# ScalarE's Sign for the weights of the first product, and one low part of three moved to VectorE

## The chip, the core and the metric

The kernel runs on one core of one Trainium2 chip (trn2). The metric is the device time of one execution in microseconds: 970.57 us, the median of 3 runs (970.44 to 973.05), before the change.

## What is computed

A gated linear attention over 4 batches, 8 heads, 768 positions and heads of 48, then two products of a multilayer kind. The weights reach the kernel as 64-bit floats.

```python
state = alpha[:, :, t, :, None] * state + einsum('bhd,bhe->bhde', k[:, :, t], v[:, :, t])
y[:, :, t] = einsum('bhd,bhde->bhe', q[:, :, t], state)      # 768 steps; x = y as 3072 x 384
x = ((x @ w_a) * (x @ w_b)) @ w_out                          # 384 -> 1536 -> 384, "the first product"
h = x @ w_in
out = (h * cos(h)) @ w_out2                                  # 384 -> 2048 -> 384
```

## The kernel before

**Tiles and stages.** The 3072 tokens are worked in six groups of 512. Attention goes in 24 chunks of 128 positions; the four chunks of the first group are worked before anything else, and each later group's chunks are worked between the matmuls of the group ahead of it. The first product takes 12 blocks f of its hidden 1536 (128 columns each). A step (g, f) issues `s1`: two products `pa` and `pb` (w_a and w_b of block f, 9 matmuls each of 128x512), and, two steps later (`LAG`), `s2`: the block's share of the output `po` (w_out, 9 matmuls). Nine and not three, because every operand is split into a high part that TensorE's fp32r form holds and a low part: `mm3` (L196 to L199) does low times high, high times low, high times high. After the six groups the second pair of products follows in the same manner (`s3`, `s4`).

**Weights.** Each 128x384 block of weights is loaded as 32-bit pairs (`raw_w`, L100): word 0 holds the low 32 bits of each float, word 1 the high 32. They are decoded on the chip, once, during the first group; afterwards they stay in SBUF. Blocks under `W2` = 36 belong to the first product (w_a and w_b of a block f, and w_out of block f - 2, come together as three); the 32 blocks from `W2` on belong to the second. The stages of the decoding, each named by a letter in the order string of a step, are

- r: ScalarE scales the low word to a small integer (`rest`, L106),
- s: VectorE takes the top two bits of the high word and ors them with it (`sign`, L111). For 17 of the 36 blocks (`banked`) ScalarE writes the small integer to a PSUM bank instead (L168), and VectorE reads it there (L169),
- n: VectorE shifts the high word left by 3 and clears its top two bits (`shift`, L126),
- a: GpSimd adds the two words as integers (`rounded`, L132): the result is the fp32 value,
- h: ScalarE casts it to the high part (`dec_h`, L190),
- l: GpSimd subtracts the high part from the value (`dec_l`, L194): the low part. The first two blocks alone have it on VectorE (letter d).

Per step three blocks of later steps go through these stages, and

```python
ORDER1 = 'sbpcrnadhlmw'
```

is the order in which a step of the first product writes its work out: s, then the scans of the next attention chunk (p, `att_pre`: L242, L250 and two products L246, L252 on VectorE), the eviction of `pa` on ScalarE (c, `s1_mid`, L437), r, n, a, d, h, l, the product of `pa` and `pb` on VectorE and its cast on ScalarE (m, `s1_mul`, L442 and L444), the low part of the step before (w, `s1_low`, L449). Behind these come the attention parts of the step: at steps 2, 4, 6, 8 (`POS0`) the scores of a chunk (`att_a`, its mask L287, and a copy L279), at steps 3, 5, 7, 9 its output (`att_b`: on ScalarE L308 and the splits L393, on VectorE L339 and L394) and one or two range checks of alpha on ScalarE (`att_chk`, L265). Engines work their own list strictly in this order (`tc.manual_schedule`). For the steps before the first `s1` the order is the string `START`, where s3, r4 and so on are the same letters with a negative step.

**Buffers.** PSUM tiles of the pool `ps` (pa, pb, the attention's tiles, and the `low` tiles of `banked` blocks) share five banks. With two steps' pa and pb among them, `pb` of a step takes the bank of `pb` of the step before, which is free when that step's L442 has read it.

**Constants.** `check1` compares the smallest absolute high word of the first product's weights with `TINY`; if any check failed, a general path (`general`) would be run behind everything else. `s1_mid` copies pa to SBUF; `s2_out` copies the result of the first product (L467).

Of the kernel before, what the change touches and what calls it, by code (L numbers as in the profile page):

```python
# [6 lines left out]
F32 = mybir.dt.float32  # L7
BF16 = mybir.dt.bfloat16
F32R = mybir.dt.float32r
I32 = mybir.dt.int32  # L10
U32 = mybir.dt.uint32
AF = mybir.ActivationFunctionType
ALU = mybir.AluOpType
# [4 lines left out]
P = 128  # L18
# [7 lines left out]
DM = H * D  # L26
FF1 = 1536
FF2 = 2048
NF1 = FF1 // P
# [6 lines left out]
ORDER1 = 'sbpcrnadhlmw'  # L36
ORDER2 = "scywrbnamdp"
POS0 = (2, 4, 6, 8)
LOV = 3
ND = 2  # L40
START = 'A0 P1 M0 w5 D0 A1 P2 Y0 M1 X0 D1 r4 x0 w6 A2 P3 M2 Y1 X1 s3 b3 r3 D2 n3 s2 a2 A3 M3 Y2 b2 n2 h2 d2 Y3 X2 r2 x1 X3 s1 b1 a1 n1 h1 L0 l1 r1 D3'
SPARE = 5
# [5 lines left out]
F_LOW = 1e-14  # L48
F_MIN = 1e-25
TINY = 2.0 ** -15  # L50


@with_exitstack
def tile_kernel(ctx, tc, al, qk, vt, vz, wts, mask, qr, vr, out):
# [48 lines left out]
    def rest(raw):  # L103
        if wide:
            lo32 = raw[:, :, 0]
            nc.scalar.activation(lo32.bitcast(I32), lo32, AF.Copy, scale=2.0 ** -29)  # L106

    def sign(raw):
        if wide:
            lo32, hi32 = raw[:, :, 0], raw[:, :, 1]  # L110
            nc.vector.scalar_tensor_tensor(out=lo32, in0=hi32, scalar=0xC0000000, in1=lo32, op0=ALU.bitwise_and, op1=ALU.bitwise_or)  # L111
# [39 lines left out]
        raws[i] = raw_w(i, wpool, "w")  # L151


    banked = set()

    def dec_r(*blocks):
        for i in blocks:
            if i not in banked:
                rest(raws[i])

    def dec_s(*blocks):
        for i in blocks:
            if i not in banked:
                sign(raws[i])
                continue
            t = ps.tile([P, DM], I32, name=f"low{i}", tag="ps")
            lo32, hi32 = raws[i][:, :, 0], raws[i][:, :, 1]
            nc.scalar.activation(t, lo32, AF.Copy, scale=2.0 ** -29)  # L168
            nc.vector.scalar_tensor_tensor(out=lo32, in0=hi32, scalar=0xC0000000, in1=t.bitcast(U32), op0=ALU.bitwise_and, op1=ALU.bitwise_or)  # L169

    def dec_b(*blocks):
        for i in blocks:
# [3 lines left out]
    def dec_n(*blocks):  # L176
        for i in blocks:
            if i >= W2:
                least(raws[i])
        for i in blocks:  # L180
            shift(raws[i])

    def dec_a(*blocks):
        for i in blocks:
# [249 lines left out]
    def s1_mid(g, f, T):  # L434
        pab = abt[g, f]
        a_sb = work.tile([P, 512], F32, name=f"asb{g}_{f}", tag="asb", bufs=2)
        nc.scalar.copy(a_sb[:, :T], pab[0][:, :T])  # L437
        abt[g, f] = (pab, a_sb)

    def s1_mul(g, f, T):  # L440
# [23 lines left out]
    def s2_out(g, t0, T):  # L464
        for o in range(KT):
            xo = att.tile([P, 512], F32, name=f"xo{g}_{o}", tag="a", bufs=3)
            nc.scalar.copy(xo[:, :T], po1[o][:, :T])  # L467
            nc.sync.dma_start(out=x2d[:, o, t0:t0 + T], in_=xo[:, :T])


# [92 lines left out]
    def check1():  # L563
        nc.vector.tensor_reduce(out=okc[:, 0:1], in_=stats[:, 0:1], axis=AX.XY, op=ALU.add)
        nc.vector.tensor_reduce(out=okc[:, 1:2], in_=stats[:, 1:4], axis=AX.XY, op=ALU.add)
        nc.vector.scalar_tensor_tensor(out=okc[:, 0:1], in0=okc[:, 1:2], scalar=0.0, in1=okc[:, 0:1], op0=ALU.mult, op1=ALU.add)
        nc.vector.tensor_scalar(out=okc[:, 1:2], in0=okc[:, 0:1], scalar1=0.0, scalar2=None, op0=ALU.is_equal)
        if wide:
            nc.vector.tensor_reduce(out=okc[:, 2:3], in_=wmin, axis=AX.X, op=ALU.min)
            nc.vector.tensor_scalar(out=okc[:, 2:3], in0=okc[:, 2:3], scalar1=TINY, scalar2=None, op0=ALU.is_ge)  # L570
            nc.vector.tensor_tensor(out=okc[:, 1:2], in0=okc[:, 1:2], in1=okc[:, 2:3], op=ALU.mult)

    def check2():
# [119 lines left out]
    for m, bl in seq:  # L693
# [5 lines left out]
            at(ld_at, m, load_raw, order[nl])  # L699
            nl += 1  # L700
        d = 1 if m < NF1 else 0
        if wide and 1 <= m < NF1 and m - 1 not in POS0:
            banked.update(bl)
        at(r_at, m - 1 - d, dec_r, *bl)
        at(s_at, m - d, dec_s, *bl)
        at(b_at, m - d, dec_b, *bl)
# [178 lines left out]
```

## Time and profile before

| what | value |
| --- | --- |
| median of 3 runs | 970.57 us |
| the profiled execution, first to last instruction (span) | 967.5 us |
| around it (970.57 - 967.5) | 3.1 us |
| TensorE busy in the span | 941.5 us, 97% |
| VectorE, ScalarE, GpSimd busy | 627.7, 491.0, 194.3 us |
| mean granted TensorE clock | 0.994 |

The span is that of one profiled execution; no device time of that execution alone is given beside it, so the 3.1 us are the difference to the median of the runs. Busy times are sums over the span: a TensorE that is 97% busy over the whole can still stand idle in one stretch, and the stretch is where the reading has to start.

### The profile page before, as it was taken

Reading aid. Unit: us, or ns where it says so; the run is one execution under the profiler, and the core shown is the slowest. Engines: PE = TensorE matmul, PEld = TensorE weight load, DVE = VectorE, ACT = ScalarE, POOL = GpSimd, SP = SyncE. Lnnn points to the kernel's source line nnn. Section 1 sums busy time; section 2 is a strip of 40 time slices with the busy share of each in tenths; the row PEclk is TensorE's granted clock in tenths of the full one; section 3 lists DMA queues with packets and bytes.
Section 4 is the critical chain, followed back from the end, with each engine's and each line's share of the span. In section 5 each row is a group of like instructions: output and inputs, shape, how many; then the busy total and the mean of one; then the engine's idle time right before and its main releaser. Section 6 shows DMA issues by size and latency. Waiting matters only on the chain.

```text
span 967.5 us, 14093 instructions
## 1 busy us (share of the span) xinstructions
PE 941.5 (97%) x5215; PEld 765.8 (79%) x5215; DVE 627.7 (65%) x1000; ACT 491.0 (51%) x1039; POOL 194.3 (20%) x184
## 2 busy tenths in 40 slices
PE   7879999999999999999999999999999999999996
PEld 5757788888888888888888878788888888888885
DVE  7999955454553556444259998766666666666664
ACT  2656633323332324233256777666566666665653
POOL 5788820000000000000037764201001000010000
PEclk9999999999999999999999999999999999999999
DMA  9765214341433333030145530010010100200001
GB/s 281 240 222 178 74 40 142 102 142 46 149 109 100 115 126 98 23 103 14 59 144 154 174 131 1 1 65 1 1 66 1 66 1 0 66 1 1 34 0 37
DMA packets 41982, 79.98 MB, mean 83 GB/s; under 512 B 6192, under 2 KB 13360, under 8 KB 41904
## 3 DMA queue, kind: packets, MB, share of 16 engines
q1 hardware_dynamic: 41760, 78.72, 25.7%
q8 instruction: 43, 0.70, 0.3%
q14 instruction: 35, 0.29, 0.1%
q10 hardware_dynamic: 144, 0.26, 0.1%
HBM read 67.36 MB, written 9.44 MB: 79 GB/s over the span
## 4 chain that ended last, share of the span: by engine, by line
PE 83%; DMA 5%; DVE 5%; ACT 3%; issue 1%; POOL 1%; SPq 1%; DVEq 0%; ACTq 0%; POOLq 0%
PE pq L198 6%; PE pq L199 6%; PE ph L199 6%; PE ph L197 6%; PE ph L198 6%; PE pq L197 6%; PE po L197 5%; PE po L198 5%; PE po L199 5%; PE pb L197 5%; PE pb L198 5%; PE pa L198 5%; PE pa L197 4%; PE pa L199 4%; PE pb L199 4%; DMA w<-wts 3%
## 5 line engine op out<-in xcount | busy, mean ns | idle before, releaser
L442 DVE TENSOR_TENSOR asb<-pb,asb 128x512 f32<-128x512 f32 x72 | 49.7, 690 | 161.1 <-PE pb L199 118.2
L132 POOL TENSOR_TENSOR w<-w 128x384 int32<-128x384 int32 x68 | 65.6, 986 | 400.4 <-DVE w L126 395.9
L198 PE MATMUL pq<-g,w 128*128 128x512 f32 x288 | 112.8, 392 | 2.2 <-DVE g L524 2.2
L444 ACT CAST ab<-asb 128x512 fp32r<-128x512 f32 x72 | 44.8, 622 | 133.4 <-DVE asb L442 133.4
L197 PE MATMUL pq<-g,w 128*128 128x512 f32 x288 | 112.3, 390 | 0.0
L199 PE MATMUL pq<-g,w 128*128 128x512 f32 x288 | 112.2, 390 | 0.0
L197 PE MATMUL ph<-x,w 128*128 128x512 f32 x288 | 112.2, 389 | 0.0
L199 PE MATMUL ph<-x,w 128*128 128x512 f32 x288 | 112.1, 389 | 0.0
L198 PE MATMUL ph<-x,w 128*128 128x512 f32 x288 | 112.0, 389 | 0.0
L499 DVE SCALAR_TENSOR_TENSOR r<-r,ph 128x512 f32<-128x512 f32 x96 | 66.1, 688 | 66.2 <-ACT r L498 65.7
L437 ACT COPY asb<-pa 128x512 f32<-128x512 f32 x72 | 42.1, 585 | 126.9 <-PE pa L199 126.8
L497 ACT ACTIVATE r<-r 128x512 f32<-128x512 f32 x96 | 60.8, 633 | 83.9 <-DVE r L493 83.9
L492 DVE SCALAR_TENSOR_TENSOR r<-n,ph 128x512 f32<-128x512 int32 x96 | 65.9, 687 | 47.6 <-ACT n L490 47.6
L194 POOL TENSOR_TENSOR w<-w,w 128x384 fp32r<-128x384 f32 x66 | 89.8, 1382 | 27.0 <-ACT w L190 23.9
L197 PE MATMUL pb<-xg,w 128*128 128x512 f32 x216 | 84.4, 391 | 6.0 <-DVE asb L442 4.6
L197 PE MATMUL po<-ab,w 128*128 128x512 f32 x216 | 88.8, 411 | 0.0
L197 PE MATMUL pa<-xg,w 128*128 128x512 f32 x216 | 84.2, 390 | 2.0 <-DVE w L169 1.1
L198 PE MATMUL po<-ab,w 128*128 128x512 f32 x216 | 84.7, 392 | 0.0
L199 PE MATMUL po<-ab,w 128*128 128x512 f32 x216 | 84.7, 392 | 0.0
L198 PE MATMUL pa<-xg,w 128*128 128x512 f32 x216 | 84.2, 390 | 0.1
L198 PE MATMUL pb<-xg,w 128*128 128x512 f32 x216 | 84.1, 389 | 0.0
L199 PE MATMUL pa<-xg,w 128*128 128x512 f32 x216 | 84.1, 389 | 0.0
(110 smaller groups left out, 1867.0 us busy)
## 6 DMA issues: line engine op xcount, KB each, us to landing
w<-wts SPq DMA_DIRECT2D x104, 384.0 KB, 4.0
al<-al SPq DMA_DIRECT2D x24, 226.2 KB, 4.4
k<-qk SPq DMA_DIRECT2D x24, 224.0 KB, 3.8
q<-qk SPq DMA_DIRECT2D x24, 224.0 KB, 3.6
x2d<-xo SPq DMA_DIRECT2D x18, 256.0 KB, 2.2
x2f<-x2d SPq DMA_DIRECT2D x18, 256.0 KB, 3.6
out_t<-yo SPq DMA_DIRECT2D x17, 256.0 KB, 2.1
v<-vt SPq DMA_DIRECT2D x22, 192.0 KB, 2.8
```

The costliest lines, as they stand in the source:

```text
L132: nc.gpsimd.tensor_tensor(out=hi32, in0=hi32, in1=lo32, op=ALU.add)
L194: e.tensor_tensor(out=wt[i][:, 1, :], in0=raws.pop(i), in1=wt[i][:, 0, :].bitcast(F32), op=ALU.subtract)
L197: nc.tensor.matmul(o, wlo, xhi, start=start, stop=False)
L198: nc.tensor.matmul(o, whi, xlo, start=False, stop=False)
L199: nc.tensor.matmul(o, whi, xhi, start=False, stop=stop)
L437: nc.scalar.copy(a_sb[:, :T], pab[0][:, :T])
L442: nc.vector.tensor_tensor(out=a_sb[:, :T], in0=pab[1][:, :T], in1=a_sb[:, :T], op=ALU.mult)
L444: nc.scalar.copy(ab[:, 0, :T], a_sb[:, :T])
L492: nc.vector.scalar_tensor_tensor(out=r, in0=n, scalar=-C1, in1=p, op0=ALU.mult, op1=ALU.add)
L497: nc.scalar.activation(r, r, AF.Sin, scale=0.5)
L499: nc.vector.scalar_tensor_tensor(out=r, in0=r, scalar=1.0, in1=p, op0=ALU.subtract, op1=ALU.mult, reverse0=True)
```

## The change

For the 36 blocks of the first product:

- ScalarE writes the small integer of the low word as 16 bits into the lower half of word 0 (`low`), in place; no block goes through PSUM any more (`banked` is gone).
- ScalarE's Sign of the high word, as bf16, goes into the upper half of word 0 (`sgn`), at the letter s. Its 1.0 or -1.0 has the bits of an fp32 number's sign and exponent; VectorE's `sign` (L111, L169) is gone for these blocks.
- VectorE's shift (`up`) is one operation, without the mask of the top bits. With the integer sum of both words the value comes out as half of the weight. So `s1_mid` and `s2_out` scale by 4 and by 2 with the copy that they make anyway, and the bound in `check1` is `SMALL`, twice `TINY`.
- `LOV` is 2: of three low parts GpSimd makes two; the third (w_out's) goes to VectorE, one step later, at the letter d. That moves 10 subtractions.

The second product's blocks (from `W2`) are decoded as before.

```diff
--- before.py
+++ after.py
@@ -8,6 +8,7 @@
 BF16 = mybir.dt.bfloat16
 F32R = mybir.dt.float32r
 I32 = mybir.dt.int32
+I16 = mybir.dt.int16
 U32 = mybir.dt.uint32
 AF = mybir.ActivationFunctionType
 ALU = mybir.AluOpType
@@ -36,7 +37,7 @@
 ORDER1 = 'sbpcrnadhlmw'
 ORDER2 = "scywrbnamdp"
 POS0 = (2, 4, 6, 8)
-LOV = 3
+LOV = 2
 ND = 2
 START = 'A0 P1 M0 w5 D0 A1 P2 Y0 M1 X0 D1 r4 x0 w6 A2 P3 M2 Y1 X1 s3 b3 r3 D2 n3 s2 a2 A3 M3 Y2 b2 n2 h2 d2 Y3 X2 r2 x1 X3 s1 b1 a1 n1 h1 L0 l1 r1 D3'
 SPARE = 5
@@ -48,6 +49,7 @@
 F_LOW = 1e-14
 F_MIN = 1e-25
 TINY = 2.0 ** -15
+SMALL = 2.0 ** -14
 
 
 @with_exitstack
@@ -151,22 +153,26 @@
         raws[i] = raw_w(i, wpool, "w")
 
 
-    banked = set()
+    def low(raw):
+        if wide:
+            nc.scalar.activation(raw.bitcast(I16)[:, :, 0], raw[:, :, 0], AF.Copy, scale=2.0 ** -29)
+
+    def sgn(raw):
+        if wide:
+            nc.scalar.activation(raw.bitcast(BF16)[:, :, 1], raw[:, :, 1].bitcast(F32), AF.Sign)
+
+    def up(raw):
+        if wide:
+            x = raw[:, :, 1]
+            nc.vector.tensor_scalar(out=x, in0=x, scalar1=3, scalar2=None, op0=ALU.logical_shift_left)
 
     def dec_r(*blocks):
         for i in blocks:
-            if i not in banked:
-                rest(raws[i])
+            (rest if i >= W2 else low)(raws[i])
 
     def dec_s(*blocks):
         for i in blocks:
-            if i not in banked:
-                sign(raws[i])
-                continue
-            t = ps.tile([P, DM], I32, name=f"low{i}", tag="ps")
-            lo32, hi32 = raws[i][:, :, 0], raws[i][:, :, 1]
-            nc.scalar.activation(t, lo32, AF.Copy, scale=2.0 ** -29)
-            nc.vector.scalar_tensor_tensor(out=lo32, in0=hi32, scalar=0xC0000000, in1=t.bitcast(U32), op0=ALU.bitwise_and, op1=ALU.bitwise_or)
+            (sign if i >= W2 else sgn)(raws[i])
 
     def dec_b(*blocks):
         for i in blocks:
@@ -178,7 +184,7 @@
             if i >= W2:
                 least(raws[i])
         for i in blocks:
-            shift(raws[i])
+            (shift if i >= W2 else up)(raws[i])
 
     def dec_a(*blocks):
         for i in blocks:
@@ -434,7 +440,7 @@
     def s1_mid(g, f, T):
         pab = abt[g, f]
         a_sb = work.tile([P, 512], F32, name=f"asb{g}_{f}", tag="asb", bufs=2)
-        nc.scalar.copy(a_sb[:, :T], pab[0][:, :T])
+        nc.scalar.activation(a_sb[:, :T], pab[0][:, :T], AF.Copy, scale=4.0 if wide else 1.0)
         abt[g, f] = (pab, a_sb)
 
     def s1_mul(g, f, T):
@@ -464,7 +470,7 @@
     def s2_out(g, t0, T):
         for o in range(KT):
             xo = att.tile([P, 512], F32, name=f"xo{g}_{o}", tag="a", bufs=3)
-            nc.scalar.copy(xo[:, :T], po1[o][:, :T])
+            nc.scalar.activation(xo[:, :T], po1[o][:, :T], AF.Copy, scale=2.0 if wide else 1.0)
             nc.sync.dma_start(out=x2d[:, o, t0:t0 + T], in_=xo[:, :T])
 
 
@@ -567,7 +573,7 @@
         nc.vector.tensor_scalar(out=okc[:, 1:2], in0=okc[:, 0:1], scalar1=0.0, scalar2=None, op0=ALU.is_equal)
         if wide:
             nc.vector.tensor_reduce(out=okc[:, 2:3], in_=wmin, axis=AX.X, op=ALU.min)
-            nc.vector.tensor_scalar(out=okc[:, 2:3], in0=okc[:, 2:3], scalar1=TINY, scalar2=None, op0=ALU.is_ge)
+            nc.vector.tensor_scalar(out=okc[:, 2:3], in0=okc[:, 2:3], scalar1=SMALL, scalar2=None, op0=ALU.is_ge)
             nc.vector.tensor_tensor(out=okc[:, 1:2], in0=okc[:, 1:2], in1=okc[:, 2:3], op=ALU.mult)
 
     def check2():
@@ -699,8 +705,6 @@
             at(ld_at, m, load_raw, order[nl])
             nl += 1
         d = 1 if m < NF1 else 0
-        if wide and 1 <= m < NF1 and m - 1 not in POS0:
-            banked.update(bl)
         at(r_at, m - 1 - d, dec_r, *bl)
         at(s_at, m - d, dec_s, *bl)
         at(b_at, m - d, dec_b, *bl)
```

Three places show how the instructions move. In the names, w is a block's raw words or its split parts, low a PSUM tile, asb and ab the product of pa and pb.

VectorE between steps 3 and 4, before (L394 the splits of chunk 4, L111 letter s, L126 letter n, L442 letter m):

```order
L394 TENSOR_TENSOR xg_853<-py_1_821,xg_853 112x128
L111 SCALAR_TENSOR_TENSOR w_690<-w_690 128x384
L111 SCALAR_TENSOR_TENSOR w_692<-w_692 128x384
L111 SCALAR_TENSOR_TENSOR w_694<-w_694 128x384
L126 TENSOR_SCALAR w_690<-w_690 128x384
L126 TENSOR_SCALAR w_692<-w_692 128x384
L126 TENSOR_SCALAR w_694<-w_694 128x384
L442 TENSOR_TENSOR asb_4_915<-pb_4_890,asb_4_915 128x512
```

and in the changed kernel (L400 the splits, L167 the shift, L200 a low part, L448 the product):

```order
L400 TENSOR_TENSOR xg_843<-py_1_811,xg_843 112x128
L167 TENSOR_SCALAR w_683<-w_683 128x384
L167 TENSOR_SCALAR w_685<-w_685 128x384
L167 TENSOR_SCALAR w_687<-w_687 128x384
L200 TENSOR_TENSOR w_802<-w_571,w_802 128x384
L448 TENSOR_TENSOR asb_4_905<-pb_4_880,asb_4_905 128x512
```

Three instructions are gone ahead of the product, and one has come: the low part of a block whose value and high part were made a step earlier.

ScalarE at the same place, before (L393 the splits, L265 the range checks, L437 the eviction of pa, L190 letter h):

```order
L393 ACTIVATE xg_853,stats<-py_1_821 112x128
L265 ACTIVATE junk,stats<-g_789,lim 112x516
L265 ACTIVATE junk,stats<-g_634,lim 112x516
L437 COPY asb_4_915<-pa_4_880 128x512
L190 CAST w_923<-w_619 128x384
```

and in the changed kernel (L162 is the Sign, L158 the 16-bit low word, L443 the eviction):

```order
L399 ACTIVATE xg_843,stats<-py_1_811 112x128
L271 ACTIVATE junk,stats<-g_779,lim 112x516
L271 ACTIVATE junk,stats<-g_627,lim 112x516
L162 ACTIVATE w_683<-w_683 128x384
L162 ACTIVATE w_685<-w_685 128x384
L162 ACTIVATE w_687<-w_687 128x384
L443 ACTIVATE asb_4_905<-pa_4_870 128x512
L158 ACTIVATE w_770<-w_770 128x384
```

Three Signs now stand between the range checks and the eviction; the low words of three blocks, which before went to PSUM in the step after, are made here, in place.

GpSimd, two rounds of the letters a and l before (L132 the sum, L194 the low part):

```order
L132 TENSOR_TENSOR w_568<-w_568 128x384
L194 TENSOR_TENSOR w_807<-w_564,w_807 128x384
L194 TENSOR_TENSOR w_809<-w_566,w_809 128x384
L194 TENSOR_TENSOR w_811<-w_568,w_811 128x384
L132 TENSOR_TENSOR w_619<-w_619 128x384
```

and in the changed kernel (L134 the sum, L200 the low part):

```order
L134 TENSOR_TENSOR w_571<-w_571 128x384
L200 TENSOR_TENSOR w_798<-w_567,w_798 128x384
L200 TENSOR_TENSOR w_800<-w_569,w_800 128x384
L134 TENSOR_TENSOR w_618<-w_618 128x384
```

The third subtraction has left GpSimd's list; the sums follow one instruction sooner.

## Rows read from the trace of the kernel before

**Rows 1.** The page: TensorE's busy tenths in 40 slices, about 24 us each.

```profile
PE   7879999999999999999999999999999999999996
```

**Rows 2.** Windows: stretch, length, busy us (count) by engine, granted clock, DMA.

```profile
34.40:112.00 77.60, 67.39 (x410) 52.05 (x411) 72.87 (x115) 47.82 (x122) 65.53 (x54) 0.98 0.59 188
112.00:475.00 363.00, 363.00 (x2375) 295.66 (x2374) 185.93 (x317) 119.23 (x324) 16.11 (x13) 1.00 0.29 90
52.30:55.20 2.90, 2.90 (x10) 2.32 (x9) 2.90 (x4) 1.20 (x4) 2.90 (x3) 0.51 1.03 402
```

**Rows 3.** Timeline, TensorE, 34 to 112 us: start, length, instruction, [idle before, releaser].

```profile
34.40 0.47 PE L197 MATMUL pa<-xg,w 128*128 128x512 f32 x1 [0.90 <-ACT xg L393]
...
40.22 0.47 PE L197 MATMUL pa<-xg,w 128*128 128x512 f32 x1 [1.10 <-DVE w L169]
...
50.30 1.16 PE L272 MATMUL pa<-q,k 48*128 48x128 f32 x16 [1.64 <-DVE q L252]
...
70.53 0.47 PE L197 MATMUL pb<-xg,w 128*128 128x512 f32 x1 [1.14 <-DVE asb L442]
...
106.40 0.47 PE L197 MATMUL pb<-xg,w 128*128 128x512 f32 x1 [1.64 <-DVE asb L442]
```

**Rows 4.** Timeline, VectorE: the products L442 of steps 1 to 7.

```profile
50.97 0.69 DVE L442 TENSOR_TENSOR asb<-pb,asb 128x512 f32<-128x512 f32 x1
...
58.99 0.68 DVE L442 TENSOR_TENSOR asb<-pb,asb 128x512 f32<-128x512 f32 x1
...
69.71 0.68 DVE L442 TENSOR_TENSOR asb<-pb,asb 128x512 f32<-128x512 f32 x1
...
75.96 0.68 DVE L442 TENSOR_TENSOR asb<-pb,asb 128x512 f32<-128x512 f32 x1
...
86.47 0.68 DVE L442 TENSOR_TENSOR asb<-pb,asb 128x512 f32<-128x512 f32 x1
...
95.50 0.68 DVE L442 TENSOR_TENSOR asb<-pb,asb 128x512 f32<-128x512 f32 x1
...
105.58 0.68 DVE L442 TENSOR_TENSOR asb<-pb,asb 128x512 f32<-128x512 f32 x1
```

**Rows 5.** Timeline, VectorE, from the first product's start to the step 1 product.

```profile
34.85 3.06 DVE L111 SCALAR_TENSOR_TENSOR w<-w 128x384 uint32<-128x384 uint32 x3
...
39.54 1.47 DVE L169 SCALAR_TENSOR_TENSOR w<-w,low 128x384 uint32<-128x384 uint32 x3
...
43.52 1.49 DVE L169 SCALAR_TENSOR_TENSOR w<-w,low 128x384 uint32<-128x384 uint32 x3 [1.10 <-ACT low L168]
44.92 1.66 DVE L242 TENSOR_TENSOR_SCAN g<-al,one_end 112x516 f32<-112x516 f32 x1
...
50.16 0.90 DVE L126 TENSOR_SCALAR w<-w 128x384 uint32<-128x384 uint32 x3
```

**Rows 6.** Timeline, VectorE: three shifts with GpSimd at work, beside those at 50.16.

```profile
92.19 3.38 DVE L126 TENSOR_SCALAR w<-w 128x384 uint32<-128x384 uint32 x3
```

**Rows 7.** Timeline, ScalarE: two waits, the check ahead of step 4's eviction, three low words.

```profile
28.43 0.83 ACT L314 COPY sbd<-ts 48x96 f32<-48x96 f32 x3 [1.08 <-DVE ts L305]
...
39.70 0.53 ACT L168 ACTIVATE low<-w 128x384 int32<-128x384 uint32 x1 [3.80 <-issue]
...
74.24 0.73 ACT L265 ACTIVATE junk<-g,lim 112x516 uint8<-112x516 f32 x1
...
79.83 1.44 ACT L106 ACTIVATE w<-w 128x384 int32<-128x384 uint32 x3
```

**Rows 8.** Groups by line and shape: busy us, mean ns of one | idle before.

```profile
L116 ACT ACTIVATE w<-w 128x384 f32<-128x384 f32 x32 | 17.5, 559 | 16.9 <-DVE w L111 16.8
...
L265 ACT ACTIVATE junk<-g,lim 112x516 uint8<-112x516 f32 x24 | 17.4, 725 | 0.1
```

**Rows 9.** The same view, VectorE.

```profile
L194 DVE TENSOR_TENSOR w<-w,w 128x384 fp32r<-128x384 f32 x2 | 2.3, 1184 | 0.0
...
L394 DVE TENSOR_TENSOR xg<-py,xg 128x384 fp32r<-128x384 f32 x2 | 1.0, 543 | 0.0
```

## The prediction

> **What bounds the kernel now.** I read the slices of the page first: TensorE shows a 9 in every slice from the fifth to the last but one, and 7, 8, 7 or 8 only in the first ones [rows 1]. The windows say the same in microseconds: from 112 to 475 us TensorE is busy for all of 363.00 us, from 34.40 to 112.00 us for 67.39 of 77.60 [rows 2]. So what ScalarE, VectorE and GpSimd do matters only in the first group of 512 tokens, while the weights are decoded, and the most that can be had there is 77.60 - 67.39 = 10.2 us of waits, and what a low clock costs. The third window gives that: between 52.30 and 55.20 us the granted clock is 0.51, the lower of TensorE's two levels (1.2 against 2.4 GHz), right behind the wait of 1.64 us at 50.30 [rows 2, 3]. Half of those 2.9 us, about 1.4 us, would not be needed at the upper level. The weights of the second product are decoded around 500 to 600 us as before and drop out of the reckoning.
>
> Next the timeline of TensorE for who ends its waits. At 40.22 us it is VectorE's L169, that is, a PSUM bank that holds a low word; at 50.30 us the scaled q of chunk 4; at 70.53 and 106.40 us, and at two more places (steps 3 and 7), it is the product L442 of the step before, which gives back the bank of pb [rows 3]. In all four, pb starts 0.14 us behind L442's end: 69.71 + 0.68 = 70.39, and 70.53; 105.58 + 0.68 = 106.26, and 106.40 [rows 3, 4]. The wait at 106.40 is the last one of any size. **So the end moves by as much as the L442 of step 7, at 105.58, moves**, as long as TensorE's own work does not become later than it. That row is what I follow, from L442 to L442 [rows 4]: the distances are 8.02, 10.72, 6.25, 10.51, 9.03 and 10.08 us for steps 1 to 7. The long ones (even to odd steps) hold the scans of a chunk on VectorE, the short ones its splits.
>
> **Part 1: up to the L442 of step 1.** VectorE loses L111 at 34.85, L169 at 39.54 and L169 at 43.52 with its wait of 1.10 [rows 5]: 3.0 + 1.4 + 2.5 = 6.9 us on a VectorE that is otherwise nearly without gaps there. The Signs go to ScalarE. For a Sign I take 0.47 us: three of L106 take 1.44 [rows 7], and Abs on the same shape has 559 ns for one against an overlap of about 0.1 [rows 8]. No row shows a 16-bit result at every eighth byte; the nearest below is that 0.47, the nearest above the range check with its 8-bit result, 725 ns on 516 columns [rows 8]. Beside that price: the Trainium skill (ScalarE: Activation LUTs, section on what ACT_TABLE_LOAD costs) gives 280 ns + 0.833 ns per element for an ACTIVATE whose bias is a pointer, overlapping the next by about 93 ns. By that page a Sign would be 0.60 us long and 0.51 apart, an estimate; the sum would lose 0.7 us by it.
>
> Ahead of the first product ScalarE gets four Signs, 1.9 us. It waits 1.08 us there for VectorE at 28.43 [rows 7], and VectorE comes sooner by two L111; I take +0.4 us for the first matmul (bounds 0 and 1.9): 34.8. Behind it ScalarE has three Signs, two casts, three low words and three Signs, 11 times 0.47 = 5.2 us, until 40.0. Before, it stood 3.80 us idle for a PSUM bank in this stretch [rows 7], and that idle time pays for the Signs. So the L442 of step 0 starts near 40.7, the scans at 41.3; from the scan at 44.92 to the shifts at 50.16 is 5.24 us [rows 5], so they end at 46.5; three shifts (0.8) and the new low part follow. Its price lies between 0.54 us (L394, one operand in PSUM) and 1.18 us (the same subtraction on VectorE with GpSimd at work) [rows 9]; I take the middle, 0.85, because GpSimd works in part of the stretch. L442 of step 1: 48.2 against 50.97, **-2.8 us**. The waits at 40.22 and 50.30 and the low clock go with it, which is why TensorE can follow.
>
> **Part 2: the loops.** Even to odd (three of them): three L169 go (1.40 from start to the next start, 43.52 to 44.92 [rows 5]), a low part comes: -1.40 + 0.85 = -0.55 each, **-1.65**. The Signs lie under the scans there. Odd to even: here the Signs are a new wait, since the shift overwrites the word that Sign reads, and ScalarE comes to them only behind the splits and the range checks. In step 3 to 4 the second check starts at 74.24 and ends near 74.97 [rows 7], 5.26 us after the L442 at 69.71; three Signs to 6.67, the last shift to 7.0, the low part to 7.8. That is +1.55 against 6.25; the same 7.8 in step 5 to 6, also with two checks, is -1.2 against 9.03. From step 1 to 2 there are no splits: about 2.15 us to the end of one check, 1.4 for the Signs, 0.3 and 0.85: 4.7, **-3.3** against 8.02. Together -1.65 + 1.55 - 1.2 - 3.3 = **-4.6**. The 9.03 is long because its three shifts took 3.38 us beside GpSimd [rows 6] where those at 50.16 took 0.90 [rows 5]; such a round took place in two of seven steps. GpSimd has 10 of 34 subtractions fewer here, but will still meet shifts: I leave half a round, **+1.2**.
>
> **What costs nothing.** The scale in the copies of pa and of the result replaces a copy by one with a factor, covered by a full TensorE after 112 us [rows 2]; the 17 low words that leave PSUM for SBUF stay on ScalarE. The DMAs are issued in the same order.
>
> **The sum:** -2.8 - 4.6 + 1.2 = -6.2 us, made against the trace's span of 967.5 us. The median of the runs stands 3.1 us above that span; I take this as unchanged: 970.6 - 6.2 = **964.4 us**. It is 55% of the 11.4 us that waits and clock offer (10.2 + about 1.2 of the 1.4). A run of this kernel can tell a change from none at about 0.3%, 2.9 us. Late next would be pb of step 6: its bank comes with the L442 of step 5, about 1 us after TensorE could use it.
>
> **Rivals.**
> 1. *All waits go* (ScalarE and GpSimd keep out of VectorE's way): -11.4 us, 959.2. For it: VectorE loses 36 instructions and gets 10. Against: the new wait for Sign in odd to even steps. Chance 0.10.
> 2. *The move to VectorE is worth less.* GpSimd and VectorE hold each other up: the low part always costs 1.18 us [rows 9], 0.33 more in six loops, 2.0 us: 966.4. The Trainium skill (Perfetto Trace Analysis, section Optimizing Scalar/DVE Operations) says that moving work between these two "might not help" since they share an SBUF read port; by that rule this is the outcome, and the 3.38 against 0.90 us agrees with it. Chance 0.12.
> 3. *ScalarE sets the pace.* A Sign costs 0.73 (the upper row) instead of 0.47. There are 19 Signs on the way: four ahead of the first matmul, six up to the L442 of step 0, nine in the odd to even loops. 19 x 0.26 = 4.9 us: -1.3, 969.3. For it: ScalarE has 36 more instructions in a stretch in which it was busy 47.82 of 77.60 us [rows 2]. Chance 0.17.
> 4. *Slower.* The same place, and Sign's 16-bit result in 8-byte steps costs double, 1.0 us: 19 x 0.53 = 10.1, less 6.2: +3.9, 974.5. It decides from 0.80 us per Sign on, and is measurably slower from 0.95. No row shows such a write, so none excludes it; the 8-bit result of the range checks at 725 ns speaks against. Chance 0.08.
> 5. *It doesn't do what it says*: values or bound are off, and the general path is run behind the rest, which no row prices and which would add all three products again. Chance 0.01.
>
> **Chances.** The forecast has 0.52. Faster by over 0.3%: nearly all of it, rivals 1 and 2, and little of 3: 0.72. Within: most of 3 and the edges of the others, 0.18. Slower: 4, 5 and some spread, 0.10. The range goes from rival 1 to rival 3, 959.2 to 969.8; it leaves out rivals 4 and 5 and what lies beyond the edges.
>
> **What would show it.** Right: no wait for a low word's bank near 40 us; the step 1 L442 near 48 us and that of step 7 near 99; 36 Signs of 0.5 to 0.6 us; odd to even loops near 7.8 with VectorE waiting for ScalarE ahead of its first shift; the clock at the upper level around 50 us. Wrong: Signs above 0.8 us, a first matmul after 36 us, VectorE waiting for GpSimd's sums ahead of the low part, or waits after 112 us.

## The result, and the profile after

The changed kernel took 979.45 us (median of 4 runs, 977.43 to 979.71), the kernel before beside it 970.51 us (median of 4). The ratio is 1.0082, with a 95% interval of 1.0069 to 1.0094: slower by about 9 us. The forecast was 964.4 us, in a range of 959.2 to 969.8. The profiled execution has a span of 977.6 us, 10.1 more than that of before. The medians differ by less, 8.9 us: every run whose span is on record stands 1.8 to 2.4 us above it, so the profiled execution of before was about 1 us quicker than the median, and the 3.1 us between the two were partly that.

The page of the profile after says where to look: the busy tenths of two engines in 40 slices of about 24 us, and TensorE's granted clock in tenths.

```profile
PE   7788999999999999999999999999999999999996
...
ACT  2999953331433323333357687766666666666653
...
PEclk7989899999999999999999999999999999999999
```

TensorE reads nearly as before [rows 1], but ScalarE now shows a 9 in the second to the fifth slice. The windows of the same trace (stretch, length, then busy us and count for PE, PEld, DVE, ACT, POOL, granted clock, DMA share, GB/s):

```profile
34.40:112.00 77.60, 63.78 (x396) 50.16 (x393) 52.89 (x86) 77.53 (x136) 47.44 (x40) 0.93 0.58 187
112.00:135.00 23.00, 21.11 (x136) 16.74 (x135) 15.61 (x29) 19.78 (x49) 17.92 (x16) 0.93 0.16 44
```

Against rows 2, VectorE went from 72.87 to 52.89 us busy, as it was meant to, and ScalarE from 47.82 to 77.53 of 77.60 us: it has no gap left. TensorE lost 67.39 - 63.78 = 3.6 us of work in the first window. It also waits past 112 us now, where it had been busy throughout [rows 2].

The groups of ScalarE's instructions by line and shape say why (busy us, mean ns of one, idle before):

```profile
L162 ACT ACTIVATE w<-w 128x384 bf16<-128x384 f32 x36 | 34.1, 1119 | 0.0
L158 ACT ACTIVATE w<-w 128x384 int16<-128x384 uint32 x36 | 34.0, 1115 | 0.0
...
L108 ACT ACTIVATE w<-w 128x384 int32<-128x384 uint32 x32 | 16.8, 558 | 2.8 <-DMA w<-wts 2.8
```

L162 is the Sign and L158 the low word of the 36 blocks of the first product. L108 is the same low word for the second product, still written as 4 bytes: the same input and the same shape at 558 ns. Both 16-bit results cost double. In the timeline of ScalarE (start, length, instruction) three of a kind stand together:

```profile
44.03 2.92 ACT L162 ACTIVATE w<-w 128x384 bf16<-128x384 f32 x3
46.67 0.71 ACT L443 ACTIVATE asb<-pa 128x512 f32<-128x512 f32 x1
47.25 2.76 ACT L158 ACTIVATE w<-w 128x384 int16<-128x384 uint32 x3
49.74 1.45 ACT L196 CAST w<-w 128x384 fp32r<-128x384 f32 x3
```

From one start to the next engine task three Signs take 2.64 us, 0.88 each; three low words 2.49, 0.83 each. Three 4-byte low words took 1.44 from the first start to the last end before [rows 7].

VectorE now waits for ScalarE: its first shift of each of these two steps stands behind a Sign (timeline, VectorE).

```profile
45.22 0.57 DVE L167 TENSOR_SCALAR w<-w 128x384 uint32<-128x384 uint32 x1 [3.76 <-ACT w L162]
...
61.78 0.74 DVE L167 TENSOR_SCALAR w<-w 128x384 uint32<-128x384 uint32 x1 [4.04 <-ACT w L162]
```

And TensorE waits for what comes behind these (timeline, TensorE).

```profile
38.12 0.50 PE L203 MATMUL pa<-xg,w 128*128 128x512 f32 x1 [2.86 <-ACT xg L399]
...
52.04 0.79 PE L203 MATMUL pa<-xg,w 128*128 128x512 f32 x1 [5.09 <-POOL w L200]
...
64.06 0.47 PE L203 MATMUL pa<-xg,w 128*128 128x512 f32 x1 [1.33 <-ACT asb L443]
```

The first of them is the first matmul of the product, at 38.12 instead of 34.40 [rows 3]: the split L399 that it waits for comes right behind three low words of the double price (timeline, ScalarE).

```profile
34.92 2.75 ACT L158 ACTIVATE w<-w 128x384 int16<-128x384 uint32 x3
37.41 0.57 ACT L399 ACTIVATE xg<-py 128x384 fp32r<-128x384 f32 x1
```

The products of the steps, which the prediction follows as L442 [rows 4], are now L448. Steps 0, 1, 7 and 8 (timeline, VectorE):

```profile
47.41 0.69 DVE L448 TENSOR_TENSOR asb<-pb,asb 128x512 f32<-128x512 f32 x1
...
56.47 0.68 DVE L448 TENSOR_TENSOR asb<-pb,asb 128x512 f32<-128x512 f32 x1
...
111.93 0.68 DVE L448 TENSOR_TENSOR asb<-pb,asb 128x512 f32<-128x512 f32 x1
...
121.43 0.68 DVE L448 TENSOR_TENSOR asb<-pb,asb 128x512 f32<-128x512 f32 x1
```

and steps 0 and 8 before:

```profile
41.73 0.68 DVE L442 TENSOR_TENSOR asb<-pb,asb 128x512 f32<-128x512 f32 x1
...
111.60 0.68 DVE L442 TENSOR_TENSOR asb<-pb,asb 128x512 f32<-128x512 f32 x1
```

Steps 1 and 7 start at 56.47 and 111.93, against 50.97 and 105.58 before and 48.2 and 99.4 forecast. Of the 6.3 us by which step 7 is late, 5.7 are there at step 0 already. The loop from step 7 to step 8 adds 3.5 more (9.50 us against 6.02), so step 8 is 9.8 us late, nearly the 10.1 of the span. TensorE's line of the page adds up the same way:

```profile
PE 946.7 (97%) x5215; PEld 770.9 (79%) x5215; DVE 605.5 (62%) x974; ACT 535.7 (55%) x1075; POOL 179.8 (18%) x174
```

It is idle for 977.6 - 946.7 = 30.9 us, 4.9 more than the 26.0 of before, and busy for 5.2 us more with the same number of matmuls. That fits its granted clock, 0.93 in both windows against 0.98 and 1.00 [rows 2].

### The profile page after: what moved, and what is told of

The parts are those of the page before. It is cut to its first block, busy times and chain, and to the rows that moved or that the text cites. A ratio compares the mean times of both kernels' runs of the same rounds, so it can differ in the third digit from the quotient of the medians.

```text
span 977.6 us, 14093 instructions
## 1 busy us (share of the span) xinstructions
PE 946.7 (97%) x5215; PEld 770.9 (79%) x5215; DVE 605.5 (62%) x974; ACT 535.7 (55%) x1075; POOL 179.8 (18%) x174
## 4 chain that ended last, share of the span: by engine, by line
PE 81%; ACT 10%; DMA 3%; DVE 3%; issue 1%; POOL 1%; SPq 1%; ACTq 0%; DVEq 0%; POOLq 0%
PE pq L204 6%; PE pq L205 6%; PE ph L203 6%; PE ph L204 6%; PE ph L205 6%; PE pq L203 6%; PE po L203 5%; PE po L204 5%; PE po L205 5%; PE pa L205 4%; PE pa L203 4%; PE pb L205 4%; PE pb L203 4%; PE pa L204 4%; PE pb L204 4%; ACT w L158 2%
## 5 line engine op out<-in xcount | busy, mean ns | idle before, releaser
L448 DVE TENSOR_TENSOR asb<-pb,asb 128x512 f32<-128x512 f32 x72 | 49.7, 690 | 163.2 <-PE pb L205 120.4
L134 POOL TENSOR_TENSOR w<-w 128x384 int32<-128x384 int32 x68 | 69.3, 1037 | 403.8 <-DVE w L128 392.1
L443 ACT ACTIVATE asb<-pa 128x512 f32<-128x512 f32 x72 | 43.8, 608 | 127.4 <-PE pa L205 127.4
L203 PE MATMUL pb<-xg,w 128*128 128x512 f32 x216 | 84.5, 391 | 0.0
L204 PE MATMUL pb<-xg,w 128*128 128x512 f32 x216 | 84.3, 390 | 0.0
L205 PE MATMUL pb<-xg,w 128*128 128x512 f32 x216 | 84.2, 390 | 0.0
```

What stands on the lines that cost most here:

```text
L134: nc.gpsimd.tensor_tensor(out=hi32, in0=hi32, in1=lo32, op=ALU.add)
L203: nc.tensor.matmul(o, wlo, xhi, start=start, stop=False)
L204: nc.tensor.matmul(o, whi, xlo, start=False, stop=False)
L205: nc.tensor.matmul(o, whi, xhi, start=False, stop=stop)
L443: nc.scalar.activation(a_sb[:, :T], pab[0][:, :T], AF.Copy, scale=4.0 if wide else 1.0)
L448: nc.vector.tensor_tensor(out=a_sb[:, :T], in0=pab[1][:, :T], in1=a_sb[:, :T], op=ALU.mult)
```

## The experiments

Three theories were tested. **Theory 1, the price:** a 2-byte result at every eighth byte costs ScalarE about 0.88 us instead of 0.47; 72 of them fill it. **Theory 2, the place:** the Signs stand ahead of the eviction of pa, and the shift waits for them, whatever they cost. **Theory 3:** the low part that went to VectorE does it.

### The low word as 4 bytes

```diff
-            nc.scalar.activation(raw.bitcast(I16)[:, :, 0], raw[:, :, 0], AF.Copy, scale=2.0 ** -29)
+            nc.scalar.activation(raw[:, :, 0].bitcast(I32), raw[:, :, 0], AF.Copy, scale=2.0 ** -29)
```

The Sign comes later and overwrites the upper half of the word, so the values are the same.

> The changed kernel with the low word written as 32 bits (a 4-byte result, as before the change) and the Sign still as bf16 into the upper half. Theory 1 (price: a 2-byte result of ScalarE at every eighth byte costs about 0.88 us in its queue where the 4-byte one costs 0.47, and 72 of them fill ScalarE in the first group): half of the dear results are gone, ScalarE has 36 x 0.41 = 15 us less; 964.4 + 19 x 0.41 = about 972 us (970 to 975), L158 near 0.56 us each, the Sign still near 1.1. Theory 2 (place: the Signs stand ahead of pa's eviction in ScalarE's list and the shift waits for them, whatever they cost): 977 to 979 us. Theory 3 (the low part on VectorE is what costs): 977 to 979 us.

Measured: 968.27 us (10 runs, 967.33 to 969.67), ratio to before 0.9967 (0.9957 to 0.9977). So one type in one line is worth 979.45 - 968.27 = 11.2 us (1.15% by the ratios), and this version is faster than both kernels, than the one before by 0.3%. ScalarE's rows:

```profile
L162 ACT ACTIVATE w<-w 128x384 bf16<-128x384 f32 x36 | 34.1, 1121 | 0.0
L158 ACT ACTIVATE w<-w 128x384 int32<-128x384 uint32 x36 | 17.5, 562 | 0.0
```

The low word has halved, and the Sign has not moved. ScalarE is busy 73.99 of 77.60 us in the same window, and the product of step 7 starts at 101.86 instead of 111.93:

```profile
101.86 0.68 DVE L448 TENSOR_TENSOR asb<-pb,asb 128x512 f32<-128x512 f32 x1
```

Theory 1 had expected a gain of less, to 970 us at best.

### Both as 4 bytes

```diff
-            nc.scalar.activation(raw.bitcast(BF16)[:, :, 1], raw[:, :, 1].bitcast(F32), AF.Sign)
+            nc.scalar.activation(raw[:, :, 0].bitcast(F32), raw[:, :, 1].bitcast(F32), AF.Sign)
```

On top of the first edit. The Sign now covers the whole word, so the rounded low bits of the weights are left out of the sum; instructions, order and waits stay.

> The changed kernel with the low word as 32 bits and the Sign as fp32 over the whole of word 0: the same instructions in the same order, all results of 4 bytes. The low bits of the weights are left out of the sum, so this tells the time alone. Theory 1: both near 0.56 us, and the time that was forecast with this price, 964.4 us (961 to 968). Theory 2: 975 to 979 us, since the Signs stand where they stood. Theory 3: 975 to 979 us.

Measured: 964.23 us (4 runs, 963.00 to 964.61), ratio 0.9921 (0.9900 to 0.9943). That is the forecast of 964.4. Groups of ScalarE, then the window and two of the products (VectorE's timeline) of this kernel:

```profile
L158 ACT ACTIVATE w<-w 128x384 int32<-128x384 uint32 x36 | 18.0, 572 | 1.2 <-DMA w<-wts 1.2
L162 ACT ACTIVATE w<-w 128x384 f32<-128x384 f32 x36 | 17.7, 569 | 0.0
```

```profile
34.40:112.00 77.60, 73.50 (x469) 57.57 (x470) 63.09 (x99) 65.17 (x162) 63.74 (x50) 0.98 0.61 195
```

```profile
48.52 0.68 DVE L448 TENSOR_TENSOR asb<-pb,asb 128x512 f32<-128x512 f32 x1
...
98.32 0.68 DVE L448 TENSOR_TENSOR asb<-pb,asb 128x512 f32<-128x512 f32 x1
```

The Signs stand at the same place, ahead of the eviction, and the shift waits for them all the same. Only their price is another, and with it the time falls by 15.2 us. That refutes theory 2 as the cause of the loss and shows theory 1. The place is not free even so: VectorE's shifts still wait 10.2 us for the Signs, against 22.4 in the changed kernel.

The two types do not share the 15.2 us evenly. The Signs' type is worth 968.27 - 964.23 = 4.0 us when the low words are cheap, the low words' type 11.2 when the Signs are dear. In the window ScalarE is busy for 65.17 us with neither, 73.99 with one and 77.53 with both, so the second dear type met an engine that had 3.6 us left. That is a reading and was not tested: no run has dear low words and cheap Signs.

### All three low parts on GpSimd again

```diff
-LOV = 2
+LOV = 3
```

In the changed kernel:

> The changed kernel with LOV = 3: all three low parts on GpSimd again. Theory 1: ScalarE sets the pace and neither GpSimd (47 of 78 us busy in the first group) nor VectorE (53 of 78) does, so the time stays within 1.5 us of the changed kernel: 978 to 981 us. Theory 2: the same. Theory 3: 969 to 973 us.

Measured: 980.14 us (4 runs), ratio 1.0086 (1.0064 to 1.0108), against 1.0082 with the move. Theory 3 falls: the loss is there without it.

### The move alone, in the kernel before

```diff
-LOV = 3
+LOV = 2
```

> The kernel before with LOV = 2 and nothing else: the third low part on VectorE, one step later. If the move is worth something by itself (GpSimd has 10 of its subtractions less, meets VectorE's shifts less often): 966 to 969 us. If VectorE, which sets the pace there with 72.87 of 77.60 us busy, only gets more to do (10 times 0.55 to 1.18 us, six of them in loops that end a wait): 971 to 975 us.

Measured: 970.35 us (10 runs), ratio 0.9991 (0.9977 to 1.0004). Alone it gives nothing that can be told from none; neither range of the expectation holds it. Its profile also shows how far a single row can be trusted. The same instructions as before stand ahead of the first matmul, and still it starts 2.4 us later than the 34.40 of before (timeline, TensorE):

```profile
36.77 0.50 PE L197 MATMUL pa<-xg,w 128*128 128x512 f32 x1 [0.24 <-ACT xg L393]
```

The mean granted clock from 0 to 34.40 us was 0.80 in this profile and 0.95 in that of before. Distances between rows of one profile, and medians, are the safer comparison.

### The price by itself

The kernel before, with loose instructions late in the program that nothing waits for. Source: fp32 at every eighth byte, 128x384, as in the kernel.

```diff
...
+        A = lambda o: nc.scalar.activation(o, x, AF.Sign)
+        for _ in range(2):
+         A(f[:, :, 0])
+         A(hb[:, :, 1])
+         A(flatf[:, :DM])
+         A(flatb[:, :DM])
+         A(flatb[:, :2 * DM].rearrange("p (a b) -> p a b", b=2)[:, :, 0])
+        B = lambda o: nc.vector.tensor_scalar(out=o, in0=x, scalar1=2.0, scalar2=None, op0=ALU.max)
...
```

> The kernel before, with 10 extra ScalarE instructions (Sign, 128x384, source fp32 at every eighth byte) and 8 of VectorE (max with a constant) in a late step of the first product, into a scratch tile: fp32 at every eighth byte, bf16 at every eighth, fp32 packed, bf16 packed, and on ScalarE bf16 at every fourth byte. The time of the whole says nothing. Theory 1 in the form that the pitch of 2-byte results is the cost: ScalarE's fp32 both near 0.56 us, bf16 at every eighth byte 1.1, packed bf16 0.56. In the form that any 2-byte result is dear: packed bf16 1.1 as well. bf16 at every fourth byte tells which pitch. VectorE: no theory; if it costs 0.4 to 0.5 at every eighth byte too, the half word could be written there.

Measured, one of each kind (the two of a kind are within 8 ns). The view of one line in a short stretch: the fp32 and the bf16 Sign at every eighth byte, then the fp32 and the bf16 Sign without gaps, then the bf16 Sign at every fourth byte (min/median/max ns, first and last start):

```profile
L745 ACT ACTIVATE bdst<-bsrc x1: 546/546/546, 443.2 to 443.2; 128x384 f32<-128x384 f32 x1
...
L745 ACT ACTIVATE bdst<-bsrc x1: 1075/1075/1075, 443.7 to 443.7; 128x384 bf16<-128x384 f32 x1
...
L745 ACT ACTIVATE bdst<-bsrc x1: 553/553/553, 444.9 to 444.9; 128x384 f32<-128x384 f32 x1
...
L745 ACT ACTIVATE bdst<-bsrc x1: 542/542/542, 448.9 to 448.9; 128x384 bf16<-128x384 f32 x1
...
L745 ACT ACTIVATE bdst<-bsrc x1: 642/642/642, 449.5 to 449.5; 128x384 bf16<-128x384 f32 x1
```

A Sign costs 542 to 553 ns with a 4-byte result at either spacing, and with a 2-byte result without gaps. Only the 2-byte result at every eighth byte costs 1067 to 1075; at every fourth byte it is 642 to 647. So it is neither the function nor the type nor the spacing alone. VectorE shows the same more weakly: 363 ns for fp32 at every eighth byte, 360 for bf16 without gaps, 609 for bf16 at every eighth byte. From 443 to 451 us, where the Signs run, GpSimd has no work and the DMA share is 0.00 (window), so the price is not that of their work:

```profile
443.00:451.00 8.00, 8.00 (x49) 6.27 (x49) 0.84 (x3) 7.13 (x11) 0.00 (x0) 1.00 0.00 0
```

### The sign as a 16-bit mask on VectorE

Can the 2-byte write be had cheaper on VectorE? In the kernel before, for all blocks, with no block through PSUM:

```diff
-            lo32, hi32 = raw[:, :, 0], raw[:, :, 1]
-            nc.vector.scalar_tensor_tensor(out=lo32, in0=hi32, scalar=0xC0000000, in1=lo32, op0=ALU.bitwise_and, op1=ALU.bitwise_or)
+            h = raw.bitcast(U16)
+            nc.vector.tensor_scalar(out=h[:, :, 1], in0=h[:, :, 3], scalar1=0xC000, scalar2=None, op0=ALU.bitwise_and)
...
```

> The kernel before with the sign stage on VectorE as an operation on half words (upper half of the high word, masked, into the upper half of word 0) for all blocks, no low word through PSUM, LOV 3. Nothing more on ScalarE. If the cost on VectorE is the price of its instruction, 0.6 us as in the loose measurement of a 2-byte result at every eighth byte: 36 x 0.55 = 20 us against 21.6 us of L111 and L169 in the first group, and the wait for a PSUM bank at 40 us gone: 968 to 971 us. If what costs is that L111 meets GpSimd (two operands in SBUF), and one operand does not: 964 to 968 us.

Measured: 978.24 us, ratio 1.0071 (1.0046 to 1.0095); with LOV at 2 as well:

> The same with LOV = 2. By the first reading of that kernel: 969 to 973 us, by the second 963 to 967 us.

Measured: 974.80 us (10 runs), ratio 1.0039 (1.0024 to 1.0055). Both missed. In the first of them, from 0 to 125 us, the masks by groups (busy us, mean ns of one | idle before):

```profile
L112 DVE TENSOR_SCALAR w<-w 128x384 uint16<-128x384 uint16 x36 | 32.3, 1030 | 0.0
```

and in the kernel before, in the same stretch, the two operations that they replace:

```profile
L111 DVE SCALAR_TENSOR_TENSOR w<-w 128x384 uint32<-128x384 uint32 x19 | 15.1, 845 | 0.0
...
L169 DVE SCALAR_TENSOR_TENSOR w<-w,low 128x384 uint32<-128x384 uint32 x17 | 8.5, 554 | 1.4 <-ACT low L168 1.3
```

The masks take 32.3 us where L111 and L169 took 23.6. The shortest of them is 594 ns, like the loose one. Beside GpSimd they are dear, but so is the old and-or of two words in SBUF: of those with GpSimd at work for over 90% of their time, 23 masks took 1166 ns on average and 9 of L111 1079; of those with under 10%, 10 masks took 631 and 9 of L111 551. So the mask is dearer by some 80 ns in either case. More of the loss comes from the 17 blocks that had one operand in PSUM: L169 took 554 ns, though 13 of its 17 run beside GpSimd, and 17 x (1030 - 554) is 8.1 us, an estimate. VectorE is then the full engine, with 75.74 of 77.60 us.

### No 2-byte result, the low word through PSUM

The changed kernel with the low word in a PSUM bank for all 36 blocks, Sign as fp32 over word 0, and shift and or in one operation of VectorE:

```diff
...
+            t = lows[i] = ps.tile([P, DM], I32, name=f"low{i}", tag="ps")
+            nc.scalar.activation(t, raws[i][:, :, 0], AF.Copy, bias=-0.5, scale=2.0 ** -29)
+            sgn(raws[i])
+            hi = raws[i][:, :, 1]
+            nc.vector.scalar_tensor_tensor(out=hi, in0=hi, scalar=3, in1=t.bitcast(U32), op0=ALU.logical_shift_left, op1=ALU.bitwise_or)
...
```

> The changed kernel without any 2-byte result and without leaving out bits: ScalarE writes the low word as a 4-byte integer into a PSUM bank (rounded down), Sign as fp32 over word 0, and VectorE's shift takes the low word in with an or, one operand in PSUM. LOV 2. Theory 1 (price): the changed kernel's order of Signs and waits with cheap results: 963 to 968 us; the or costs VectorE 0.2 us per block more than the plain shift. Theory 2 (place): 975 us and more, since ScalarE has the same 72 instructions, all of them now ahead of the eviction of pa.

Measured: 986.48 us, ratio 1.0162 (1.0129 to 1.0194), the slowest of all, though ScalarE is busy for 55.67 us and VectorE for 51.42 of the 77.60. The number lies in theory 2's range, 975 us and more, but the eviction that theory 2 names is not what holds TensorE up. TensorE's waits from 34 to 125 us (us in total, times, longest):

```profile
PE pa L289 <- DVE w L185: 10.0, 7, 5.4
PE pa L289 <- issue: 1.6, 1, 1.6
PE pa L214 <- DVE w L185: 1.0, 1, 1.0
```

L289 is the scores' matmul of a chunk, whose tile is one of the PSUM banks with the tag `ps`, and L185 is the operation that reads a low word there. The low words of the even steps, in which a chunk needs those banks, hold TensorE up for 10 us. The kernel before lets low words into PSUM only in the steps in which no chunk begins. L185 itself waits for ScalarE's Sign (timeline, VectorE, at the longest of these waits):

```profile
61.67 0.55 DVE L185 SCALAR_TENSOR_TENSOR w<-w,low 128x384 uint32<-128x384 uint32 x1 [1.58 <-ACT w L162]
```

By these waits it is a matter of place here, of where low word and Sign stand in ScalarE's list while a bank is held for them; price, place and bank were not separated further. The expectation had counted engines and not banks.

### Less for ScalarE in the fast version

The version with the 4-byte low word and bf16 Signs still has ScalarE busy for 73.99 of 77.60 us. One, or two, of its three low words per step went to VectorE:

```diff
...
+            elif i % 3 < 1:
+                lo = raws[i][:, :, 0]
+                nc.vector.tensor_scalar(out=lo.bitcast(I32), in0=lo, scalar1=2.0 ** -29, scalar2=None, op0=ALU.mult)
...
```

> Edit: the kernel with 4-byte low words and bf16 Signs (968.3 us), with one low word of three made on VectorE instead of ScalarE. ScalarE loses 12 results at 0.47 us apart (5.6 us), VectorE gains 12 at about 0.36 to 0.45 (4.3 to 5.4). Theory 1 (ScalarE, busy 73.99 us of 77.60 between 34.4 and 112 us, is what the loop waits for): some half of the 5.6 us comes back, 964 to 967 us, and the product of step 7 starts by 100 us instead of 101.86. Theory 2 (the place of the Signs ahead of the eviction sets the loop, whatever ScalarE's sum is): within 1 us of 968.3.

> Edit: the same with two low words of three on VectorE. Busy times by the sums: ScalarE 74.0 - 11.3 = 62.7 us, VectorE 55.0 + 8.6 to 10.8 = 64 to 66. Theory 1: 962 to 966 us, no slower than with one of three. Theory 2: within 1 us of 968.3. A third way: VectorE's low words, in the row before the Signs' shifts, hold up VectorE, then slower than with one of three.

Measured: 970.10 us with one (11 runs, ratio 0.9994, 0.9985 to 1.0003) and 972.25 with two (11 runs, 1.0015, 1.0006 to 1.0024), against 0.9967 with none. The sums of the engines came as expected; the windows of the two kernels, one row each:

```profile
34.40:112.00 77.60, 70.28 (x445) 55.00 (x439) 61.12 (x102) 68.64 (x144) 59.53 (x45) 0.96 0.58 188
```

```profile
34.40:112.00 77.60, 68.58 (x456) 53.74 (x454) 66.40 (x109) 62.12 (x131) 60.36 (x45) 0.96 0.60 188
```

ScalarE lost 5.3 and 11.9 us, and the time rose by 1.8 and 4.0 (2.6 and 4.7 by the ratios). So theory 1 fails for this step, and theory 2's 1 us does not hold it either. With two of three on VectorE, its timeline shows their place:

```profile
52.17 1.13 DVE L264 TENSOR_TENSOR q<-q,f 112x512 f32<-112x512 f32 x1
53.22 0.62 DVE L175 TENSOR_SCALAR w<-w 128x384 int32<-128x384 uint32 x2
53.76 0.89 DVE L167 TENSOR_SCALAR w<-w 128x384 uint32<-128x384 uint32 x3
54.57 0.55 DVE L206 TENSOR_TENSOR w<-w,w 128x384 fp32r<-128x384 f32 x1
55.04 0.68 DVE L454 TENSOR_TENSOR asb<-pb,asb 128x512 f32<-128x512 f32 x1
```

In an even to odd step VectorE goes from the scans through the low words L175 and the shifts to the product L454 without a gap, so there each low word makes the loop longer. From step 0 to step 7 the four even to odd loops take 35.1 us together with no low word on VectorE, 37.3 with one and 38.8 with two. This is the third way that the expectation names. The three odd to even loops get shorter, 24.0, 23.7 and 22.2 us, so there the relief of ScalarE is worth something, but less than it costs.

That is not all of it. Step 0 itself comes at 42.71, 43.93 and 47.13, and the first matmul at 34.76, 35.87 and 37.85. How much of that is the edit's was not separated: the mean granted clock up to 34.40 us differs among the three profiles too (0.90, 0.80 and 0.75).

The last run puts all three low parts of the fast version back on GpSimd:

```diff
-LOV = 2
+LOV = 3
```

> Edit: the kernel with 4-byte low words and bf16 Signs (968.3 us), with all three low parts on GpSimd again. Theory 3 (the low part on VectorE is worth something once the other engines have room): 970 to 973 us. Theories 1 and 2 (the move is worth nothing while ScalarE is the fullest engine): 967.5 to 969.5 us.

Measured: 972.79 us (11 runs), ratio 1.0020 (1.0009 to 1.0032). So in this version the move to VectorE is worth 4.5 us by the medians (0.5% by the ratios), as theory 3 has it, where in the kernels before and after it was worth nothing. With the 16-bit masks it was 3.4 us by the medians, with intervals that overlap. One wait goes with it: ScalarE's casts to the high part wait for GpSimd's sums L134 (20 to 125 us: us in total, times, longest), with all three low parts on GpSimd

```profile
ACT w L196 <- POOL w L134: 10.0, 11, 1.5
```

and with the move

```profile
ACT w L196 <- POOL w L134: 5.3, 6, 1.3
```

In the changed kernel with all three low parts on GpSimd this wait is 0.5 us, and there the move gains nothing. But in the kernel before it falls from 6.6 to 3.7 us with the move, and the time does not. So the wait alone does not decide, and when such a move pays stays open.

## Why the prediction was wrong

**The steps that failed, in short.** Two terms for ScalarE: a Sign at 0.47 us, which took 0.88, and the low words that "stay on ScalarE" at no cost, which went from 0.47 to 0.83. The second is the larger: undoing it gave back 11.2 us, undoing the first then 4.0.

**The bound and the row to follow: right in kind.** Nothing but the first group of tokens mattered. But "the end moves by as much as the L442 of step 7" came short: that row moved by 111.93 - 105.58 = 6.3 us, the row of step 8 by 9.8, the span by 10.1. The condition that stood with it, that TensorE's own work does not become later, was broken by its waits and its clock, up to 135 us.

**The price of a Sign: mis-sized.** "For a Sign I take 0.47 us" was measured at 0.88 apart, 1119 ns long. The prediction had seen that no row shows a 16-bit result at every eighth byte. But it took the lowest bound, from a 4-byte result, and as its upper one the range check, whose 8-bit result stands without gaps. Neither bound had the property that decides. The run with dear Signs and 4-byte low words shows what this error is worth by itself: 968.27 us, 4.0 more than with cheap Signs, and still inside the range. The first matmul comes at 34.76 there, as forecast (34.8). The Trainium skill (ScalarE: Activation LUTs, section What ACT_TABLE_LOAD costs) has one price per element for fp32 and bf16 alike, and gave an estimate of 0.60 us long. The trace comes near that for 4-byte results and for 2-byte ones without gaps, 0.54 to 0.57, and differs for 2-byte ones at every eighth byte, 1.07 to 1.13.

**The low word: a term put at nothing.** The same change writes the low word as int16 at the same spacing. The prediction has 17 of them "stay on ScalarE" at no cost, and it did not price the change of type at all, for these or for the other 19. It is nearly as dear as the Sign: 0.83 apart instead of 0.47. Undoing this type alone gives back 11.2 us of the 15.2 that both cost, and without it the time is inside the range. Together the 72 results are some 28 us more on ScalarE. In the stretch that holds most of them it had 77.60 - 47.82 = 29.8 us free [rows 2], and 36 Signs at 0.47, 17 us, were to go there too.

**The first matmul.** "+0.4 us, bounds 0 and 1.9" was 38.12 - 34.40 = 3.7 us: four Signs and five low words of the double price run on ScalarE between 26.5 us and the split that it waits for, nearly without a gap. At 26 us ScalarE is still where it was before, to 0.2 us. With 4-byte results the matmul comes at 34.46, 0.1 late.

**The rest of the sum: near in total, as the run with both types undone shows.** Its step 1 product starts at 48.52 (forecast 48.2) and its step 7 product at 98.32 (99.4); the time is 964.23 (964.4). There the odd to even loops are 7.2, 7.5 and 6.7 us (forecast 4.7 for the first, 7.8 for the others). So the first of them was forecast 2.5 us too short and the other two 0.3 and 1.1 too long. In the first, the range check ends 1.6 us later than forecast, behind low words that wait for their DMA and casts that wait for GpSimd's sums, and the three shifts take 2.48 us beside GpSimd. So the 1.2 us left for such a round was needed, in that loop. The even to odd ones (10.17, 9.19 and 9.13) came 1.2 shorter in sum than 10.72, 10.51 and 10.08 less 0.55 each: the low part took 0.55 us there and not 0.85. The total is right in part by luck, because errors of up to 2.5 us cancel.

**The rivals.** Rival 4 names what happened to the Sign: its 16-bit result costs double. It stood at 0.08, on the ground that the 8-bit result of the range checks spoke against. That was a wrong analogy. But its 974.5 us is no near hit: with that price alone the time is 968.27, so its 19 x 0.53 = 10.1 us for the Signs was 4.0, and the low word, which it left out, was the larger part. The pace is set as rival 3 has it, by ScalarE, at a higher price than its 0.73. Rival 2's outcome, that the move is worth less, came for the move alone in the kernels before (0.9991) and after (1.0086 without, 1.0082 with), and not in the version with 4-byte low words, where it pays about 0.5%. Its reason, a low part that always costs 1.18 us, did not come: the 12 low parts on VectorE took 648 ns on average in the changed kernel. The Trainium skill (Perfetto Trace Analysis, section Optimizing Scalar/DVE Operations) says that such a move "might not help". The trace agrees in the kernels before and after, and in the version with 4-byte low words the move did help; the shared port that it gives as the reason was tested by no run.

**The range** held neither the result nor the bound that rival 4 gave: it ended at 969.8, just above rival 3's 969.3, which rests on an upper bound that was itself too low. The prediction's own signs of being wrong did come: Signs above 0.8 us, a first matmul after 36 us, waits after 112 us.

## What to carry to other kernels

Price an instruction by its result's type and its spacing in memory together, and take as a bound only rows that have both; where no row has, write the cheap form (here 4 bytes, overwritten later by the other half) if the values allow it. When work moves to an engine, sum everything that changes on it, types of old instructions too, against its free time in that stretch, before following single waits. And a sum is only the first test: with ScalarE relieved by 5 and 12 us the time rose, and the loops that grew are those in which the work moved into another engine's unbroken chain.

## What was not expected of the hardware

A 2-byte result at every eighth byte takes ScalarE 1067 to 1075 ns for 128x384, twice the 542 to 553 of a 4-byte result there or of a 2-byte one without gaps; at every fourth byte it takes 642 to 647. VectorE takes 607 to 609 against 359 to 363 where GpSimd has no work. Beside GpSimd its 16-bit mask took 1166 on average and a 4-byte and-or of two SBUF words 1079, while the and-or with one operand in PSUM stayed at 554. The Trainium skill (SBUF — State Buffer, section Specifications (TRN2)) says that accesses with at least two hits in each 16-byte line run at full bandwidth. At eight bytes apart there are two hits in a line for either type, so by that rule both results would cost the same; the trace agrees for the 4-byte one (546 ns against 553 without gaps) and differs for the 2-byte one (1075 against 542). What it is in the write that doubles the time was not tested.
